# A fused attention and gated feed-forward kernel: another written order for tiles 3 to 8, with multiplies and block sums shared otherwise between VectorE and GpSimd

## The chip, the cores and the metric

The kernel runs on one core of a Trainium2 chip. Its time is device microseconds of one execution. The engines are TensorE (PE: matmuls; PEld: its weight loads), VectorE (DVE), ScalarE (ACT), GpSimd (POOL) and SyncE (SP, which only issues transfers). ACT and POOL issue transfers too, each in its own queue and in the order written. The median of three runs before the change is 351.02 us (351.01 to 351.19).

## The reference

Blockwise causal attention over 8 batches and 8 heads, 576 positions of 64 numbers, in blocks of 64; then a feed-forward layer with a gate over all 4608 tokens.

```python
scores = scale * np.matmul(q, k.transpose(0, 1, 3, 2))
mask = block_i >= block_j                    # blocks of 64 positions
attn = softmax(np.where(mask, scores, -1e9))
x = heads_side_by_side(np.matmul(attn, v))   # 4608 x 512
gate = np.maximum(x @ w_gate, 0.0)           # w_gate, w_val: 512 x 1536
out = (gate * (x @ w_val)) @ w_out           # w_out: 1536 x 512
```

(The names softmax and heads_side_by_side stand for a few lines of numpy.) Inputs and output are float32.

## The kernel before

The feed-forward layer is done in nine tiles of 512 tokens: tile j below 8 has the first 512 positions of batch j, and tile 8 the last 64 positions of all eight batches. Attention for batch j+1 is done in the same stretch as tile j of the feed-forward layer, so that TensorE has matmuls of the one while the other engines finish steps of the other. Tiles 0 to 2 are written in ORDER_0 (line 64), which the change leaves alone. Tiles 3 to 6 all follow ORDER_3_6 (line 85), tile 7 ORDER_7 and tile 8 ORDER_8; tiles 7 and 8 have no attention beside them.

An order is a list of short names. The loop at the end of the kernel calls do(name) for each (line 1417), and each call writes some instructions, so the list sets the order of every engine's queue: nothing is rearranged afterwards. A star and a number repeat a name. A name in a dictionary ONLY is written in tile 6 alone, and loads for a later batch (l, w, d) are left out in tile 6. These names matter here:

- g5, v5 and the like (plain, line 1327): one of four steps of a gate or value block, a matmul of 128x512. r is its relu on ACT (line 1325), h its multiply on DVE (line 1426).
- p, a pair number n from 0 to 5, then 1 to 7: one half of one of seven block products that stand for the eight of a pair of gate and value blocks (times, line 1339; matmuls of 128x256 at line 1354). Their results go through PSUM and are put together by pair (line 1372): a, u and w are copies from PSUM to SBUF on ACT (line 1376); d, e and c add a PSUM block to an SBUF one on DVE (line 1380); r is a relu on ACT. H multiplies relu and value into hT (line 1392; both inputs in SBUF; DVE, or POOL if its name is in ON_POOL), and L does relu and multiply in one on DVE (line 1396).
- X and Y: sums of blocks of x, both inputs in SBUF (x_sums, line 1162; DVE or POOL). U: sums of weight blocks (line 979).
- s and four digits: sums of blocks of hT that the output products need (make_part, line 1020; both inputs in SBUF; DVE or POOL).
- M1 to M7: the seven products of the output matrix, each in six steps of two matmuls (line 1061). oa, ou, ow and oy copy the results out on ACT (line 1106), od, oe and oc add on DVE (line 1100), S0, S1, S2 issue the stores of 256 KB from ACT's queue (line 893; line 906 in tile 8, where the stores are shared out among ACT, SP and POOL). P issues the store that the tile before left over.
- A and a number: the score matmuls of one pair of heads (visit, line 608; matmuls at line 631). E and that number with t, u, f or s: its four exponentials on ACT (lines 643 and 636). C: the zeros in the corners of the exponentials (line 1507 on DVE, 1510 on POOL). V: the products with v for one head (lines 779 and 793). N: its normalisation on DVE, a reciprocal and two multiplies (lines 716, 718, 725). T: the transposing transfer of the result into x, from SP's queue (line 862). K and k: scores of the last keys and their exponential.
- l and w: loads of q, k and v of the batch after the next, issued by POOL (line 509; each issue takes it 0.62 to 0.96 us). d: the transposing transfers of q and k from SP's queue (line 519 and after).

PSUM has eight banks of 512 columns: two pairs called sc, one called one, three called ffnp. SLOTS (line 44) says by hand which buffer each use takes. A matmul that begins a new block in a bank waits until the last reader of the earlier block has finished. That is why a late copy, exponential or add holds up TensorE. PAIR_BANK, OUT_BANK and AV_BANK (lines 140, 181, 190) choose the bank for each product. on() picks the engine by the set ON_POOL (line 170):

```python
    def on(name):
        return nc.gpsimd if name in ON_POOL else nc.vector
```

Of the kernel before, what the change touches and what calls it, by code (L numbers as in the profile page):

```python
# [17 lines left out]
def kernel(  # L18
# [24 lines left out]
    OBS = 5  # L43
    SLOTS = {
        "sc": (
            "010101010101010010101010101010101010101010101010101010101010011011001001"
            "010100110110010010101001101100100101010011011001001010011101100"
        ),
        "ffnp": (
            "021021021020210210210210210210120210120202010101210120201201120120210211"  # L50
            "201021102101020120120120121201202101202101202101210221200102021010101212"
            "011210020101202020212102212001020210101012120112100201012020202121010200"
            "21210121202011"
        ),
        "ob": (
            "043210432104314013240324103420340213241302341234120324031234023402132413"
            "023412342134120142103421"
        ),
        "gate_sb": (
            "021021021021021021021021021021021021021210201202012102121020120201210212"  # L60
            "02102102"
        ),
    }
    ORDER_0 = """
# [36 lines left out]
        p06 p0w p04 p17*2 p04 p21 p1u p0u p0e p21 p05 p15 p05 p1w p14 p31 p22 p15 p14
        p0d p03*2 p2a p22 p0r p0L p1d p31 p3a p26*2 p2c p1e p1L p13*2 p1r p27 p32 p27
        p36 p51 p37 p1H p2u p2w p37 p36 p32 p51 p3c p25*2 p2d p24 p3u p24 p2e p5a p3w
        p35 p41 p35 p3d p2L p41 p23*2 p2r p56*2 p5u p34*2 p3e p4a p3L p33*2 p3r p3H
# [8 lines left out]
        p0w p0d p1u p2a p14*2 p1e p15*2 p1d p1L p02 p03*2 p0r p26 p04 p0H p02 p31 p0c
        p31 p04 p0e p26 p13 p22 p32 p13 p0L p3a p2u p1r p22 p2c p1H s0102 p27*2 p25 p37
        p25 p2w p2d p37 P p3w p24 p36 p24 p2e p2L p36 p41 p3u s0002 p32 p3c p23*2 p2r
        p51 p41 p34 p51 p4a p35*2 p3d p34 p5a p47 p42 p56 p47 p4w p46 p33*2 p42 p3r p3e
# [43 lines left out]
        (7, 3): ('one', 'sc', 'ffn'),  # L160
        (7, 4): ('ffn', 'one', 'ffn'),
        (7, 5): ('sc', 'ffn', 'sc'),
        (8, 0): ('sc', 'ffn', 'one'),
        (8, 1): ('ffn', 'ffn', 'one'),
        (8, 2): ('sc', 'ffn', 'sc'),
# [4 lines left out]
    ON_POOL = set(  # L170
        """
        32H 3C00 3C10 3C11 3C21 3C31 3X4 3X5 3X7 3s0102 3s0302 3s1002 3s1302
        3s2202 42H 4C00 4C10 4C11 4C21 4C31 4X4 4X5 4X7 4s0102 4s0302 4s1002
        4s1302 4s2202 52H 5C00 5C10 5C11 5C21 5C31 5X4 5X5 5X7 5s0102 5s0302
        5s1002 5s1302 5s2202 62H 6C00 6C10 6C11 6C21 6C31 6X4 6X5 6X7 6s0102
        6s0302 6s1002 6s1302 6s2202 70H 72H 7X4 7X5 7X7 7Y5 7Y6 7s0102 7s1002
        7s1102 7s1202 7s2302 80H 81H 82H 83H 8s0102 8s1102 8s1202 U05 U06 U07
        U43
        """.split()
    )  # L180
# [858 lines left out]
    def seven_products(j, quads, sums):  # L1039
# [45 lines left out]
        def products(which):  # L1085
# [229 lines left out]
    def program(j):  # L1315
# [101 lines left out]
        def do(t):  # L1417
# [390 lines left out]
```

## Time and profile before

| what | value |
|---|---|
| median of three runs | 351.02 us |
| the profiled execution's own time | 350.91 us |
| its span, first to last instruction | 349.1 us |
| DVE instructions, busy | 562, 245.8 us |
| ACT instructions, busy | 348, 211.4 us |
| POOL instructions, busy | 248, 201.4 us |
| tile 3 starts, last matmul ends | 138.83 us, 343.87 us |

The profile page gives busy time by engine, 40 equal slices of the span, the chain of work that ended last, and the costliest groups of instructions. In a group or in the list of instructions by time, a line reads: start and duration in us, engine, line of the kernel, operation, output and inputs by the program's names, shape, count, and in brackets how long the engine was idle before and what ended that. A matmul's drawn end is modelled, and matmuls overlap in the pipeline; their starts are measured.

### The profile page before, as it was taken

The numbers are of one execution on the slowest core, as the hardware profiler recorded it, in microseconds if no ns is written. First come the engines' busy times: TensorE is split into PE (matmuls) and PEld (weight loads), VectorE is DVE, ScalarE is ACT, GpSimd is POOL, SyncE is SP. The second block draws the span as 40 slices with busy tenths as digits, with TensorE's granted clock in tenths as the row PEclk, the third lists the DMA queues.
The fourth block names the chain that finished last, engine by engine and source line by source line (L and its number), as shares of the span: only waits on it lengthen the run. The fifth ranks groups of instructions, "written<-read, shape, count | busy, mean of one in ns | idle before, by whom it ended". The sixth has DMA issues, their size and how long they took to land.

```text
span 349.1 us, 8920 instructions
## 1 busy us (share of the span) xinstructions
PE 338.3 (97%) x3518; PEld 233.4 (67%) x3518; DVE 245.8 (70%) x562; ACT 211.4 (61%) x348; POOL 201.4 (58%) x248
## 2 busy tenths in 40 slices
PE   8999999999999999999999999999999999999993
PEld 3544455545445568776867686777777798888873
DVE  4853455667538787589648973898379877986981
ACT  5933766687235862878278846786387727536630
POOL 2767556588867803885588755973525372531520
PEclk9999999999999999999999999999999999999999
DMA  8999999999999994999989997995710130002004
GB/s 242 295 353 373 355 235 269 217 131 185 183 235 81 143 180 82 179 130 90 108 162 151 92 116 146 151 125 100 151 32 2 34 100 31 32 0 92 32 17 103
DMA packets 155402, 50.06 MB, mean 143 GB/s; under 512 B 134465, under 2 KB 151745, under 8 KB 155361
## 3 DMA queue, kind: packets, MB, share of 16 engines
q1 hardware_dynamic: 77520, 32.52, 44.3%
q0 software_dynamic: 70528, 8.98, 44.0%
q10 hardware_dynamic: 7312, 8.00, 7.8%
q8 instruction: 27, 0.44, 0.6%
q14 instruction: 15, 0.11, 0.1%
HBM read 37.75 MB, written 9.44 MB: 135 GB/s over the span
## 4 chain that ended last, share of the span: by engine, by line
PE 76%; DMA 10%; DVE 4%; POOL 4%; ACT 3%; issue 1%; ACTq 0%; SPq 0%; POOLq 0%; DVEq 0%
PE ffnp L1170 11%; PE ffnp L1061 10%; PE ffnp L1354 10%; PE sc L1354 7%; PE sc L1061 6%; PE ffnp L1330 6%; PE ffnp L1273 5%; PE one L1354 4%; PE sc L631 3%; DMA stage<-in_moe_w_out_dram 3%; DMA stage<-in_moe_w_val_dram 2%; DMA stage<-in_moe_w_gate_dram 2%; PE ffnp L779 2%; PE one L631 2%; PE sc L779 1%; PE one L779 1%
## 5 line engine op out<-in xcount | busy, mean ns | idle before, releaser
L636 ACT ACTIVATE attnT<-sc 128x1024 bf16<-128x1024 f32 x56 | 56.8, 1037 | 0.7 <-PE sc L631 0.7
L1170 PE MATMUL ffnp<-xT,wg 128*128 128x512 bf16 x140 | 37.8, 379 | 0.0
L1180 ACT ACTIVATE gate_sb<-ffnp 128x512 bf16<-128x512 f32 x35 | 20.5, 599 | 26.8 <-PE ffnp L1170 26.7
L1106 ACT COPY ob<-ffnp 128x512 f32<-128x512 f32 x20 | 11.8, 590 | 39.1 <-PE ffnp L1061 34.9
L1061 PEld LDWEIGHTS <-stage 128*128 128x128 bf16 x336 | 31.6, 98 | 4.9 <-DVE stage L1020 1.2
L1170 PE MATMUL ffnp<-xT,wv 128*128 128x512 bf16 x112 | 32.0, 380 | 0.0
L1354 PEld LDWEIGHTS <-stage 128*128 128x128 bf16 x288 | 27.6, 98 | 6.5 <-issue 0.4
L779 PEld LDWEIGHTS <-attnT 128*128 128x128 bf16 x640 | 26.2, 98 | 7.1 <-DVE attnT L1507 1.1
L1380 DVE TENSOR_TENSOR ob<-ffnp,ob 128x512 f32<-128x512 f32 x29 | 19.8, 683 | 15.0 <-ACT ob L1376 14.5
L1510 POOL MEMSET attnT<- 64x256 bf16 x22 | 7.3, 336 | 39.0 <-ACT attnT L636 19.7
L1190 DVE TENSOR_TENSOR hT<-gate_sb,ffnp 128x512 bf16<-128x512 bf16 x28 | 19.2, 684 | 14.9 <-PE ffnp L1170 13.3
L1061 PEld LDWEIGHTS <-hT 128*128 128x128 bf16 x252 | 24.2, 98 | 5.3 <-DVE hT L1396 1.2
L1325 ACT ACTIVATE gate_sb<-ffnp 128x512 bf16<-128x512 f32 x30 | 18.3, 609 | 14.9 <-PE ffnp L1354 11.1
L1354 PEld LDWEIGHTS <-wg 128*128 128x128 bf16 x224 | 21.6, 98 | 8.0 <-issue 2.1
L509 POOL DMA_DIRECT2D v_bf<-in_v_dram x30 | 24.8, 856 | 2.4 <-DMA q_bt<-in_q_dram 1.1
L1354 PEld LDWEIGHTS <-wv 128*128 128x128 bf16 x224 | 21.6, 98 | 5.5 <-ACT attnT L636 0.5
L1273 PE MATMUL ffnp<-wo,hT 128*128 128x512 bf16 x96 | 23.8, 379 | 0.1
L1170 PEld LDWEIGHTS <-wg 128*128 128x128 bf16 x144 | 13.4, 98 | 13.8 <-issue 0.5
L1170 PEld LDWEIGHTS <-wv 128*128 128x128 bf16 x144 | 13.0, 98 | 14.3 <-issue 1.5
L509 POOL DMA_DIRECT2D q_bf<-in_q_dram x20 | 17.9, 905 | 6.2 <-DVE recip L752 5.4
L1354 PE MATMUL ffnp<-xT,wg 128*128 128x256 bf16 x124 | 21.1, 273 | 0.0
L1330 PE MATMUL ffnp<-xT,wv 128*128 128x512 bf16 x64 | 21.1, 380 | 0.0
(227 smaller groups left out, 920.0 us busy)
## 6 DMA issues: line engine op xcount, KB each, us to landing
out_dram<-ob ACTq DMA_DIRECT2D x28, 256.0 KB, 3.4
stage<-in_moe_w_val_dram SPq DMA_DIRECT2D x6, 512.0 KB, 8.7
stage<-in_moe_w_gate_dram SPq DMA_DIRECT2D x6, 512.0 KB, 8.2
stage<-in_moe_w_out_dram SPq DMA_DIRECT2D x6, 512.0 KB, 10.5
q_bf<-in_q_dram POOLq DMA_DIRECT2D x20, 128.0 KB, 4.9
k_bf<-in_k_dram POOLq DMA_DIRECT2D x20, 128.0 KB, 5.9
v_bf<-in_v_dram POOLq DMA_DIRECT2D x20, 128.0 KB, 6.9
stage<-in_v_dram SPq DMA_DIRECT2D x19, 128.0 KB, 5.4
```

Of the source, the lines that this page charges most:

```text
L509: ins = nc.gpsimd.dma_start(dst, part_of)
L636: return lambda: nc.scalar.activation(at[:, :, lo : lo + 512], sc, AF.Exp, scale=scale)
L779: nc.tensor.matmul(av[:, p, :], at[:, col : col + 128], v_bf[b % 2][:, c, h, :], start=(p == 0), stop=(c == p), skip_group_check=True,)
L1061: nc.tensor.matmul(to, sums.of(c)[which][:, 128 * p : 128 * p + 128], right, start=first, stop=(c == 5), skip_group_check=True,)
L1170: nc.tensor.matmul(to, (wg, wv)[t][f // 4][:, c, 128 * (f % 4) : 128 * (f % 4) + 128], x[:, c], start=(c == 0), stop=(c == 3),)
L1180: nc.scalar.activation(gate_sb, gate, AF.Relu)
L1190: nc.vector.tensor_tensor(out=h, in0=gate_sb, in1=val, op=AX.mult)
L1273: nc.tensor.matmul(op, hT[f][:, 128 * s : 128 * (s + 1)], wo[f // 4][:, f % 4, n0:n1], start=(f == 0), stop=(f == 11),)
L1325: nc.scalar.activation(st[key], of, AF.Relu)
L1330: nc.tensor.matmul(to, (wg, wv)[t][f // 4][:, c, 128 * (f % 4) : 128 * (f % 4) + 128], x[:, c], start=(c == 0), stop=(c == 3),)
L1354: nc.tensor.matmul(st[key][:, 256 * k : 256 * k + 256], left[:, c, 128 * k : 128 * k + 128], right[:, c], start=new and (k, c) == (0, 0), ...
L1380: nc.vector.tensor_tensor(out=t, in0=st[n, of], in1=t, op=AX.add)
```

## The change

Three things change together, and nothing else in the code does. The orders of tiles 3 to 8 are written anew; the same names stand in them, each as often as before. ON_POOL has other members: in tiles 3 to 6 the multiply 5H, the sums s0202 and s2302, X6, and the corners C01 and C20 go to POOL, while s0102, s2202, X4, X7, C00 and C10 go to DVE; U07 goes to DVE, U45 and U46 to POOL. In tile 7 the multiplies 1H and 3H, s0002 and s0302 go to POOL and X7, Y5, Y6 and s1202 to DVE; in tile 8 s1002 takes the place of s1102 on POOL. The tables of PSUM buffers and banks are fitted to the new order.

```diff
@@ SLOTS: buffers of sc, ffnp, ob and gate_sb from tile 3 on @@
...
     ORDER_3_6 = """
-        A0 E0u X5 X7 g0 g1*3 X6 X4 g0 p12*2 p11*2 g1 g0*2 E0f E0s p1a p1c p17*2 p16 w0
-        E0t C01 r0 K k p16 p1u C00 V00 N00 U05 l0 v1*2 p15*2 p1w p1d V01 N01 l1 l2 l3 r1
-        v0 p14*2 p1e p13*2 v0 p1L P p1r w1 l4 l5 A1 E1t E1u E1s v1*2 h1 p21 p22 p21 v0
-        p2a p22 v0 U45 l6 l7 C11 w2 p1H p27*2 p31 p26 U46 w3 p2c h0 E1f C10 p26 p31
-        p37*2 p2w p24*2 p2u g8 p25 p2e p25 p2d p3a p36 g8 p36 p3u V11 p2L p23*2 p35*2
-        s0002 N11 p3w p3d U06 p2r g8 p34*2 p3e g8 r8 p32*2 p3c s0202 p3L p33*2 U07 w4
-        p2H p3r p3H A2 E2u p51*2 v8*2 p52 v8 p57 v8 p57 h8 E2t p5a p56 p52 p5c p56 E2s
-        V10 p5w p5u p54*2 p5e g9*4 p55*2 d0 E2f C20 l8 w5 N10 T1 r9 A3 E3u T0 d1 d2 v9*3
-        p5L s0102 M1 v9 p5d p53*2 E3s h9 s1102 M1*3 C21 p5r p5H E3f C30 M1 V21 s1002
-        s2102 s1202 s2002 M1 E3t V20 N21 N20 s0302 M7*2 T2 M7*3 oa M6 M7 ow C31 V31 N31
-        s2202 V30 M6 N30 M6 M4*2 M6*3 M4 U47 s2302 ou M4*3 U43 oe M5*3 T3 M5*3 od S2 S1
-        M2*6 M3 s1302 U03 M3*5 oy l9 l10 d3 oc S0
+        X5 A0 E0u E0s E0f g0*2 p12 g1 p12 g1 l0 X7 X6 X4 l1 l2 l3 p11*2 p1a g0*2 C00 p1c
+        E0t r0 g1 p17*2 p16 g1 K k p16 C01 V00 N00 v1*2 p1u p15*2 p1w p1d V01 N01 p14*2
+        p1e p1L v1 p13*2 v0*2 A1 P v1 r1 h1 p1r v0 p21 E1t E1u v0 h0 E1s p21 p2a p22*2
+        p2c p31 E1f p27 g8*2 p27 p2w p26*2 p2u U45 p1H s0002 p37 p31 p3a C10 p24*2 p2e
+        p32 p25*2 p2d l4 l5 l6 w0 l7 l8 s0202 C11 p2L w1 g8 p36*2 p3u V11 N11 p37 p3w g8
+        r8 p35*2 p3d p23*2 p2r p34*2 p3e p32 p33*2 p3r p3c A2 E2t p51*2 v8*2 p57*2 E2u
+        p52*2 p2H l9 l10 s0102 p3L p5a w2 w3 p3H s1002 p5c v8 p56 v8 h8 p56 p5w E2s C21
+        p54*2 U05 p5u p5e g9 E2f g9*3 r9 V10 N10 p55*2 p5d p5L v9*2 A3 E3t E3u v9*2 h9
+        d0 d1 T0 T1 d2 p53*2 p5r C20 U46 V20 M1 p5H s1102 N20 s2102 s2002 s1202 s2202
+        E3f V21 M1*3 M7*2 M1*2 E3s C30 M7*2 C31 N21 d3 T2 w4 s1302 s2302 U07 w5 oa M7*2
+        ow M6*2 V30 N30 M6*4 V31 N31 T3 M4*2 ou M5*6 U06 od M4*4 oe S1 M2 U03 s0302 M3*6
+        oy S0 U47 U43 M2*5 S2 oc
     """
@@ ORDER_7 and ORDER_8: their ends alone @@
-        p42*2 p52*2 p5c p4c p46*2 p57 p4u p57 p47*2 p55*2 p5w p5d p4w p45*2 p4d p44*2
-        p4e p54*2 p5e M1 p43 M2*2 p53*2 p4L p5L p0H s0002 P p43 p4r p4H p5r p5H M1*3 M2
-        M1*2 M2*2 s0202 s2002 s0102 M2 M7 oa M6 s2202 s2102 p2H s1102 s1002 s1202 M6 M7
+        p3e p3L p52*2 p3r p5u p5w p42 p5c p42 p4c p3H p55*2 p5d p46 p47 p54 p47 p4u p54
+        p5e p4w p45*2 p4d M2 p44*2 p4e p53*2 M1*2 p5L p4L p5r p43 M2 p43 p4r p5H s0202
+        p4H s2002 M1*2 M7 s1002 s1202 M1*2 M2*3 s2202 s1102 M7 M2 oa M6*6 s2102 M7*4 P
...
-        p3L p2H p46 p4u p56 p5u M2 p44*2 s0202 p4c p4e p52 p45 p57*2 p55*2 p45 p3H s1002
-        p4L p5w p5d p52 p4d p54*2 p5e p5c p5L p53*2 M1 p5r p5H p43*2 p4r p4H M7 M2 M1*5
-        oa s2002 s2202 M2 oca Sa s1202 M2*3 M6*6 ou s2102 s1102 M7*2 s0302 ocb s2302
+        s0102 p4c p46 p4u p44 p52*2 p5c p56 p44 p4e p57*2 p2H p45*2 p4d p5u p55*2 p5w
+        p5d M7 p54*2 p5e M1 p43 M1 p53*2 M2*2 p5r p4L p43 p4r p5L M1*4 oa p5H p4H s2002
+        s2202 M2*4 p3H s1002 s1102 s2302 s2102 s1202 M6*5 M7 M6 ou s0302 ocb Sb oca M7*4
...
@@ ON_POOL: its first lines, tile 3 @@
-        32H 3C00 3C10 3C11 3C21 3C31 3X4 3X5 3X7 3s0102 3s0302 3s1002 3s1302
-        3s2202 42H 4C00 4C10 4C11 4C21 4C31 4X4 4X5 4X7 4s0102 4s0302 4s1002
+        32H 35H 3C01 3C11 3C20 3C21 3C31 3X5 3X6 3s0202 3s0302 3s1002 3s1302
+        3s2302 42H 45H 4C01 4C11 4C20 4C21 4C31 4X5 4X6 4s0202 4s0302 4s1002
...
-    AV_BANK = {0: ('ffn', 'one'), 1: ('sc', 'sc'), 2: ('ffn', 'sc'), 3: ('ffn', 'one')}
+    AV_BANK = {0: ('ffn', 'one'), 1: ('sc', 'sc'), 2: ('ffn', 'ffn'), 3: ('ffn', 'sc')}
```

More of the change, by code (lines that the diff above doesn't have):

```diff
@@ L45 @@
         "sc": (
-            "010101010101010010101010101010101010101010101010101010101010011011001001"
-            "010100110110010010101001101100100101010011011001001010011101100"
+            "010101010101010010101010101010101010101010101010101010101001100100110101"
+            "10011001001101011001100100110101100110010011010110001010101"
         ),
@@ L50 @@
             "021021021020210210210210210210120210120202010101210120201201120120210211"
-            "201021102101020120120120121201202101202101202101210221200102021010101212"
-            "011210020101202020212102212001020210101012120112100201012020202121010200"
-            "21210121202011"
+            "201021102101020120120120121201202101202101202101210201021201021001001201"
+            "201020121020120020021021020102120102100100120120102012102012002002102100"
+            "0201210210021210102"
         ),
         "ob": (
-            "043210432104314013240324103420340213241302341234120324031234023402132413"
-            "023412342134120142103421"
+            "043210432104314013240312402312301243021340231230124302134023123012430213"
+            "402312302130214201240312"
         ),
         "gate_sb": (
-            "021021021021021021021021021021021021021210201202012102121020120201210212"
-            "02102102"
+            "021021021021021021021021021021021021021201012010212102120101201021210210"
+            "21021021"
         ),
@@ L98 @@
+        p54*2 U05 p5u p5e g9 E2f g9*3 r9 V10 N10 p55*2 p5d p5L v9*2 A3 E3t E3u v9*2 h9
[3 more added lines that the diff above has]
+        oy S0 U47 U43 M2*5 S2 oc
     """
     ORDER_7 = """
-        p11*2 p1a p01 p02 p01 X5 X7 X6 p07 p0a p12 p07 p12 X4 p1c p02 p0c Y5 p16 p06 p16
@@ L101 @@
[L101 to L104, printed above, removed]
-        p42*2 p52*2 p5c p4c p46*2 p57 p4u p57 p47*2 p55*2 p5w p5d p4w p45*2 p4d p44*2
-        p4e p54*2 p5e M1 p43 M2*2 p53*2 p4L p5L p0H s0002 P p43 p4r p4H p5r p5H M1*3 M2
@@ L107 @@
-        M1*2 M2*2 s0202 s2002 s0102 M2 M7 oa M6 s2202 s2102 p2H s1102 s1002 s1202 M6 M7
-        M6*4 ou M7*4 ow M5*5 M4 M5 s0302 s1302 od S2 M4*5 oe M3*2 s2302 M3 S1 M3 Y7 Y6
-        oc M3*2 oy S0
+        X5 p11*2 p1a p01*2 p0a X7 X6 p21 p02 p12*2 p1c X4 p07*2 p16 p02 p06 p0c p16 p06
+        p0w p04*2 p21 p22 p0u p0e p1u p05*2 p0d p22 p15 p17 p0L p2a p2c p17 p15 p1w p1d
+        p03*2 p26 p0r p0H p31*2 p14 p27 p3a p27 p14 p1e p13 p37 p13 p1r p1H s0002 p1L
+        s0102 p36 p26 p36 p32*2 p3c Y5 p51*2 p37 p2u p25 p2w p25 p2d p24*2 p2e p5a p56
@@ L110 @@
+        p3u p35*2 p23 p41 p23 p41 p3w p3d p2r p2H p34*2 p57 p33*2 p57 p56 p2L p4a p46
+        p3e p3L p52*2 p3r p5u p5w p42 p5c p42 p4c p3H p55*2 p5d p46 p47 p54 p47 p4u p54
+        p5e p4w p45*2 p4d M2 p44*2 p4e p53*2 M1*2 p5L p4L p5r p43 M2 p43 p4r p5H s0202
+        p4H s2002 M1*2 M7 s1002 s1202 M1*2 M2*3 s2202 s1102 M7 M2 oa M6*6 s2102 M7*4 P
+        ou M5*6 s2302 Y7 s0302 s1302 ow od S2 M4*5 oc M4 oe M3*6 oy S1 S0 Y6
     """
     ORDER_8 = """
-        p01*2 p11*2 p12 p0a p17*2 p1a p1w p07*2 p06*2 p12 p21*2 X4 p1c p16*2 p0u p05*2
@@ L113 @@
[L113 to L116, printed above, removed]
-        p3L p2H p46 p4u p56 p5u M2 p44*2 s0202 p4c p4e p52 p45 p57*2 p55*2 p45 p3H s1002
-        p4L p5w p5d p52 p4d p54*2 p5e p5c p5L p53*2 M1 p5r p5H p43*2 p4r p4H M7 M2 M1*5
@@ L119 @@
-        oa s2002 s2202 M2 oca Sa s1202 M2*3 M6*6 ou s2102 s1102 M7*2 s0302 ocb s2302
-        M7*3 ow M5*4 Sb M5*2 od s1302 S2 M4*6 M3*6 oy S0 oe S1
+        X4 p01 p17 p07 p21 p01 p07 p11*2 p17 p12 p21 p12 p0a p06 p1a p1c p06 p16*2 p0w
+        p04*2 p0u p05 p0e p05 p0d p1u p15*2 p1w p14 p1d p14 p1e p1L p31*2 p02*2 p0c p03
+        p2a p3a p03 p0r p0H p13*2 p1r p1H p26*2 p2u p27*2 p0L p41*2 p32*2 p3c p25 p36
+        p2w p25 p36 p2d p24*2 p2e p4a p3u p37 p22*2 p2c p37 p23*2 p3w p2r p51*2 s0002
@@ L121 @@
+        p2L p35*2 p3d p42 P p5a p34*2 p3e p3L p42 p47*2 p4w p33*2 p56 p46 p3r s0202
+        s0102 p4c p46 p4u p44 p52*2 p5c p56 p44 p4e p57*2 p2H p45*2 p4d p5u p55*2 p5w
+        p5d M7 p54*2 p5e M1 p43 M1 p53*2 M2*2 p5r p4L p43 p4r p5L M1*4 oa p5H p4H s2002
+        s2202 M2*4 p3H s1002 s1102 s2302 s2102 s1202 M6*5 M7 M6 ou s0302 ocb Sb oca M7*4
+        M5*5 ow M4 M5 M4*3 od S2 M4*2 s1302 M3*4 Sa M3*2 oy S0 oe S1
     """
@@ L156 @@
         (6, 5): ('ffn', 'one', 'ffn'),
-        (7, 0): ('ffn', 'ffn', 'ffn'),
-        (7, 1): ('sc', 'sc', 'one'),
+        (7, 0): ('ffn', 'one', 'sc'),
+        (7, 1): ('sc', 'sc', 'ffn'),
         (7, 2): ('ffn', 'ffn', 'ffn'),
[L160 to L165, printed above, removed]
+        (7, 3): ('one', 'ffn', 'sc'),
+        (7, 4): ('sc', 'ffn', 'one'),
+        (7, 5): ('sc', 'ffn', 'ffn'),
+        (8, 0): ('sc', 'one', 'one'),
+        (8, 1): ('ffn', 'ffn', 'ffn'),
+        (8, 2): ('sc', 'ffn', 'one'),
         (8, 3): ('ffn', 'ffn', 'one'),
         (8, 4): ('sc', 'sc', 'one'),
-        (8, 5): ('ffn', 'one', 'ffn'),
+        (8, 5): ('ffn', 'ffn', 'ffn'),
     }
@@ L171 @@
         """
-        32H 3C00 3C10 3C11 3C21 3C31 3X4 3X5 3X7 3s0102 3s0302 3s1002 3s1302
-        3s2202 42H 4C00 4C10 4C11 4C21 4C31 4X4 4X5 4X7 4s0102 4s0302 4s1002
[L174 to L178, printed above, removed]
+        32H 35H 3C01 3C11 3C20 3C21 3C31 3X5 3X6 3s0202 3s0302 3s1002 3s1302
+        3s2302 42H 45H 4C01 4C11 4C20 4C21 4C31 4X5 4X6 4s0202 4s0302 4s1002
+        4s1302 4s2302 52H 55H 5C01 5C11 5C20 5C21 5C31 5X5 5X6 5s0202 5s0302
+        5s1002 5s1302 5s2302 62H 65H 6C01 6C11 6C20 6C21 6C31 6X5 6X6 6s0202
+        6s0302 6s1002 6s1302 6s2302 70H 71H 72H 73H 7X4 7X5 7s0002 7s0102 7s0302
+        7s1002 7s1102 7s2302 80H 81H 82H 83H 8s0102 8s1002 8s1202 U05 U06 U43
+        U45 U46
         """.split()
     )
-    OUT_BANK = {(2, 'v'): 'ffn', (2, 'w'): 'ffn', (2, 'x'): 'one', (3, 'v'): 'sc', (3, 'w'): 'ffn', (3, 'x'): 'sc', (4, 'v'): 'sc', (4, 'w'): 'ffn', (4, 'x'): 'sc', (5, 'v'): 'sc', (5, 'w'): 'ffn', (5, 'x'): 'sc', (6, 'v'): 'sc', (6, 'w'): 'ffn', (6, 'x'): 'sc', (7, 'v'): 'ffn', (7, 'w'): 'ffn', (7, 'x'): 'one', (8, 'v'): 'one', (8, 'w'): 'sc', (8, 'x'): 'one'}
+    OUT_BANK = {(2, 'v'): 'ffn', (2, 'w'): 'ffn', (2, 'x'): 'one', (3, 'v'): 'sc', (3, 'w'): 'one', (3, 'x'): 'ffn', (4, 'v'): 'sc', (4, 'w'): 'one', (4, 'x'): 'ffn', (5, 'v'): 'sc', (5, 'w'): 'one', (5, 'x'): 'ffn', (6, 'v'): 'sc', (6, 'w'): 'one', (6, 'x'): 'ffn', (7, 'v'): 'sc', (7, 'w'): 'ffn', (7, 'x'): 'ffn', (8, 'v'): 'one', (8, 'w'): 'ffn', (8, 'x'): 'one'}
     UP_MEM = {
```

## The prediction

> **What bounds the kernel now.** I read the busy line and the 40 slices of the page first, then the shares of the chain, then the busy time of each tile of work, and last the instructions in order of time around the places where TensorE comes late.
>
> ```profile
> PE 338.3 (97%) x3518; PEld 233.4 (67%) x3518; DVE 245.8 (70%) x562; ACT 211.4 (61%) x348; POOL 201.4 (58%) x248
> ...
> PE   8999999999999999999999999999999999999993
> ...
> PEclk9999999999999999999999999999999999999999
> ...
> PE 76%; DMA 10%; DVE 4%; POOL 4%; ACT 3%; issue 1%; ACTq 0%; SPq 0%; POOLq 0%; DVEq 0%
> ```
>
> TensorE (PE) is the bound: busy 97%, clock granted in full. So the change can only remove or add gaps between matmuls. 97% hides small gaps, since a matmul is drawn about 0.16 us longer than the step to the next one. I therefore count steps from start to start. Rows of "x4" 128x256 matmuls of mean 0.273 last 0.60, a step of 0.109; 13 of 128x512 last 2.81, a step of 0.216; ten 128x65 last 0.48, a step of 0.03.
>
> Tiles 3 to 6 hold 196 of the first (21.4 us), 32 of the second (6.9), 120 of the third (3.6), four score visits of 0.77 (3.1) and last_keys (0.1): about 35.2 us. Tiles 7 and 8 hold 252 of the first: 27.5. The stretches from the start of one tile to the next:
>
> ```profile
> core 0: us, PE busy (x) PEld busy (x) DVE busy (x) ACT busy (x) POOL busy (x), PEclk, DMA share, GB/s
> 138.83:175.33 36.50, 36.23 (x417) 27.54 (x417) 26.66 (x60) 24.67 (x41) 24.73 (x30) 1.00 1.36 128
> 175.33:212.37 37.04, 36.52 (x417) 27.50 (x418) 27.61 (x62) 24.75 (x41) 27.21 (x32) 1.00 1.37 132
> 212.37:249.65 37.28, 36.58 (x418) 27.48 (x418) 27.57 (x62) 24.85 (x41) 25.96 (x31) 1.00 1.27 128
> 249.65:286.23 36.58, 36.28 (x418) 27.63 (x418) 29.00 (x66) 24.75 (x41) 16.48 (x19) 1.00 0.19 48
> 286.23:315.09 28.86, 28.29 (x255) 24.38 (x253) 23.99 (x39) 15.04 (x28) 11.73 (x10) 1.00 0.11 38
> ```
>
> Lost against these sums: 1.3, 1.8, 2.1, 1.4 and 1.4 us, and 1.3 in tile 8 (315.09 to the last matmul's end at 343.87): 9.3 us, all that the written order can win. Of it 7.0 us stand at few places, named below; 2.3 are scattered.
>
> **What late means here.** The first matmul of p11 in tile 4:
>
> ```profile
> 175.44 0.58 ACT L1106 COPY ob<-ffnp 128x512 f32<-128x512 f32 x1 [4.22 <-PE ffnp L1061]
> ...
> 176.05 0.38 ACTq L893 DMA_DIRECT2D out_dram<-ob  x1
> ...
> 176.48 0.60 ACT L643 ACTIVATE attnT<-ffnp 128x512 bf16<-128x512 f32 x1 [0.46 <-PE sc L631]
> 176.97 1.94 ACT L636 ACTIVATE attnT<-sc 128x1024 bf16<-128x1024 f32 x2
> ...
> 177.19 0.60 PE L1354 MATMUL ffnp<-xT,wg 128*128 128x256 bf16 x4
> 178.04 0.60 PE L1354 MATMUL sc<-xT,wg 128*128 128x256 bf16 x4 [0.25 <-ACT attnT L636]
> ```
>
> Four matmuls from 177.19 would let the next start at 177.63; it starts at 178.04, 0.41 late, because its PSUM bank is freed by an exponential that stands behind oy (0.58) and the issue of the store S0 (0.38) on ACT. The second kind of delay is two engines that meet:
>
> ```profile
> 193.26 1.23 DVE L1020 TENSOR_TENSOR stage<-stage,hT 128x512 bf16<-128x512 bf16 x1
> ...
> 194.48 1.63 POOL L1020 TENSOR_TENSOR stage<-hT 128x512 bf16<-128x512 bf16 x1
> ...
> 195.02 1.64 DVE L1392 TENSOR_TENSOR hT<-gate_sb,ob 128x512 bf16<-128x512 bf16 x1
> ```
>
> A block sum (L1020) takes 0.42 on DVE elsewhere and 1.16 on POOL, a multiply (L1392) 0.68 on DVE. Here the multiply p3H beside POOL's sum s0102 takes 1.64, and A3, behind it on DVE, is 0.39 late (g9 just before, 0.19). The Trainium skill ("SBUF — State Buffer", section "Who interferes with whom") says that a VectorE instruction with two SBUF inputs contends with a GpSimd instruction that reads SBUF, and whichever issues first holds the port to its end; these three lines agree.
>
> **The change, part by part.** No matmul is added or removed, and tiles 0 to 2 are untouched. I count each wait of PE as a chain: the matmul that releases the first operation, the operations in their written order, the matmul that waits. Operations queued back to back start 0.08 (DVE) or 0.12 (ACT) before the earlier one's drawn end. On the old order this gives 0.44 for p11 (measured 0.41), 0.18 for A1 (0.18), 1.18 in tile 7 (1.19) and 1.00 in tile 8 (1.02), so I use it on the new one.
>
> 1. *Start of tiles 4 to 6.* Old: M3 ends, then oy 0.59, S0 0.38, E0u 0.60, E0f 1.03, while PE has 2.46 us up to p11; short by 0.44. New: M2*5 and S2 stand between; oy, S0, S2 (0.38), E0u, E0s against 3.33 us of PE: slack 0.02. last_keys (K), 0.13 late in each of these tiles, gets slack 0.11. Lost now 3 x 0.54 = 1.6; I leave 0.1. **-1.5.**
> 2. *A1.* Its second bank waits for p15, p1d 0.69, three steps of N01 (0.19, 0.42, 0.21), p1e 0.69. The new order has one more half of v (0.216) between: from 0.18 late to 0.03 to spare, four tiles. **-0.7.**
> 3. *g9 and A3.* Lost now 0.19 twice, and 0.40, 0.39, 0.39, 0.19: 1.75. s0202 goes to POOL and earlier in the order, s0102 to DVE, so that POOL's queue near p3H holds load issues (l9, l10, w2, w3) and no sum in tiles 3 to 5; DVE also gives away p5H (0.68). Multiplies beside load issues kept 0.68 (p1H in tiles 3 to 5). The chains to A3 get slack 0.36. I leave 0.1 in all. **-1.65.**
> 4. *V11, the added wait.* Corner C11 now stands on POOL behind s0202: A1, E1t 0.60, E1u 0.60, E1s 1.03, p2a 0.59, p2c 0.69, p1H 0.69, s0002 0.42, then POOL 1.15 and 0.31, against 5.93 us of PE: short by 0.12. The old tile 5 lost 0.37 at the same matmul, behind load issues. Queued behind C11 on POOL: w1 and 2H, both with over 2 us to spare. Bounds 0 and, if s0202 takes the 1.63 that s0102 took, 0.6 a tile. I take 0.17, near the counted chain. 0.68 against 0.37: **+0.3.**
> 5. *5H on POOL.* p53, p5r 0.60, 5H 1.16, s2102 0.42, M7: slack 0.11; on DVE 5H cost 0.68. M7 loses 0.09 a tile now. Bounds 0 and 1.4 a tile (third rival); I take 0.14, since nothing that reads two SBUF tiles is written beside 5H on DVE but s1102, which ends before it. **+0.2.**
> 6. *X4 and X7 to DVE, X6 to POOL.* DVE's sums of 0.42 now stand beside the load issues l1 and l2, as s0202 did beside l8 and w5 when it took 1.23. Bounds 0 and 0.8 each; DVE has over 1 us with nothing to do before p1c (waiting for E0u, E0s, E0f and p1a), which covers either end: **0**. Uncovered it would be 0.8 a tile.
> 7. *Tile 7.* Up to M6 the new chain is p54, seven long DVE operations (0.69, step 0.60), four sums (step 0.34), with ends and semaphores 6.1 us against 5.34 of PE: 0.78 for 1.19. **-0.4.**
> 8. *Tile 8.* Old: nine long and three short operations from p44, 7.2 against 6.21. New: seven long and two short from p45, 5.55 against 5.12: 0.44 for 1.02. **-0.6.**
> 9. *Transfers.* Transposes T2 and T3 land 3.4 to 4.0 after issue; the new chain to p12 (V31, two steps of N31, T3, landing) keeps 2.2 us. d0 and d1 (4.5 and 1.8 of SP's queue) now stand ahead of T0 on SP, and T0 is still over 5 us early. The last stores keep their number, size and order (landing 2.0 to 2.7 after issue): **0**.
>
> Sum: -1.5 - 0.7 - 1.65 + 0.3 + 0.2 - 0.4 - 0.6 = -4.35. The profiled execution took 350.91 us (span 349.1 and 1.8 around it), the median of the runs is 351.02: **346.7 us**.
>
> **Rivals.** *Half of it is eaten by GpSimd's new queue.* V11 waits for POOL, and s0202 shares the port with whatever DVE does: at the upper bound of step 4 it is 0.6 - 0.17 = 0.43 a tile more, with tile 6, where s2202 meets s1302 (+0.47), 2.2 us: 348.9. For it speaks the 0.37 of tile 5, against it that DVE has only PSUM-fed adds (p2e, p2d) beside s0202; those kept 0.67 to 0.69 in all 84 cases.
>
> *The order only trades stalls.* The waits with counted slack of 0.02 to 0.11 (p11, K, A1, M7, four tiles, some sixteen places) each come 0.25 late: +4: within 0.2% of 351.0. Against it: the old order has seven places of 0.00 to 0.12 in each tile (p27, p34 to p36, p33, A3, M5), and only A3, where GpSimd meets DVE, shows a gap.
>
> *Slower: the shared port at the end of the tile.* If 5H on POOL runs a little later than counted it meets s2102 and, in turn, s1302 meets s2202 and s1102; each of these sums then takes 1.24 instead of 0.42, and V30, behind them on DVE, comes 1.43 late: 4 x 1.4 = 5.7 us: 352.4. It decides the sign from 1.1 us a tile. By the skill's rule above, read strictly, every such meeting costs the whole of GpSimd's instruction, which is this case. Against it: old s2102 and s1202 ran at 0.42 next to POOL's memset, and all three would have to meet in each tile.
>
> **How the numbers follow.** Forecast 346.7, own range 345.3 to 348.2: 0.62. First rival, 348.9 (348.2 to 350.3): 0.22. Traded stalls: 0.08. Slower: 0.08. About 0.2% (0.7 us) is what a measurement here can tell from no change. Lower end: the scattered losses of V11, M7 and tile 7 gone as well, 345.3; upper end, most of the first rival, 349.8. Faster 0.84, same 0.08, slower 0.08.
>
> **What would show it.** Tiles 3 to 6 of 35.7 to 36.1 us each, 7 and 8 of some 28.3; p11, K and A1 start without a gap; no p3H over 0.8 on DVE in tiles 3 to 5; V11's wait on POOL's L1510 in each tile at 0.1 to 0.3; M6 late by 0.8 and 0.4 in tiles 7 and 8. I am wrong if DVE's sums around s2102 take over 1 us, if V11 loses 0.5 or more, or if an xT transpose ends a wait of PE.

## The result and the profile after

The median of four runs after the change is 347.19 us (346.79 to 348.30), against 351.04 us (351.01 to 351.19) for the kernel before: a ratio of 0.9895, 95% interval 0.987 to 0.992. 3.85 us are won; 4.35 were forecast, and 347.19 lies inside the range.

The profiled execution after is the longest of the four: 348.30 us, span 346.5. From its page (the trace has 3477 of the 3518 matmuls, and all of their weight loads, by which I place them):

```profile
PE 333.9 (96%) x3477; PEld 234.0 (68%) x3518; DVE 239.8 (69%) x561; ACT 211.2 (61%) x348; POOL 202.4 (58%) x249
...
PEclk9999999999999999999999999999999999999999
...
PE 84%; ACT 4%; DVE 3%; DMA 3%; ACTq 2%; issue 2%; SPq 0%; POOL 0%; DVEq 0%
```

The clock is as before. In the chain of work that ended last PE rises from 76% to 84%, and POOL, 4% before, is gone. ACTq, which was 0%, has 2%: the queue of ACT's own transfers is on the chain now. Tiles 4, 5 and 7, from the start of each to the start of the next:

```profile
core 0: us, PE busy (x) PEld busy (x) DVE busy (x) ACT busy (x) POOL busy (x), PEclk, DMA share, GB/s
...
175.29:212.01 36.72, 35.67 (x413) 27.46 (x418) 25.74 (x61) 24.73 (x41) 25.58 (x33) 1.00 1.26 128
212.01:248.00 35.99, 35.56 (x412) 27.44 (x416) 25.75 (x61) 24.80 (x41) 24.76 (x31) 1.00 1.45 132
...
283.78:312.63 28.85, 27.97 (x254) 24.47 (x252) 25.24 (x42) 14.75 (x27) 13.47 (x11) 1.00 0.11 37
```

Tiles 3, 5 and 6 (35.95, 35.99, 35.78) are inside the promised 35.7 to 36.1. Tile 4 took 36.72, and tile 7 28.85 where 28.3 was promised. Counted from the start of tile 3 to the span's end, 210.27 us became 207.16; the stretch ahead of tile 3, which the change does not touch, was 0.51 longer in this execution.

The new losses, read as before from the distance between the starts of matmuls. At the start of tile 4:

```profile
174.92 1.68 ACTq L892 DMA_DIRECT2D out_dram<-ob  x2
...
176.65 0.60 ACT L642 ACTIVATE attnT<-ffnp 128x512 bf16<-128x512 f32 x1 [1.76 <-PE sc L630]
...
177.29 0.38 PE L1329 MATMUL ffnp<-xT,wg 128*128 128x512 bf16 x1 [0.41 <-ACT attnT L642]
...
178.21 0.60 PE L1353 MATMUL sc<-xT,wg 128*128 128x256 bf16 x4 [0.32 <-ACT attnT L635]
```

The issues of S0 and S2 take 1.68 us together (0.39 and 1.25), so E0u starts at 176.65; g1 is 0.58 late for it and p11 0.27. At the start of tile 5 the same pair took 0.38 and 0.48, and nothing waits there. At the start of tile 7 the second issue took 1.81, and p16 is 0.50 late.

The meeting of engines that the prediction showed in tile 4 is gone. DVE and POOL at the same place after:

```profile
193.80 0.54 DVE L1019 TENSOR_TENSOR stage<-hT 128x512 bf16<-128x512 bf16 x1
...
194.00 1.28 POOL L508 DMA_DIRECT2D k_bt<-in_k_dram  x2
...
194.86 0.68 DVE L1391 TENSOR_TENSOR hT<-gate_sb,ob 128x512 bf16<-128x512 bf16 x1
...
195.26 0.92 POOL L508 DMA_DIRECT2D v_bf<-in_v_dram  x1
```

The multiply p3H takes 0.68 where it took 1.64; s0102, now on DVE, takes 0.54 (2H ends on POOL 0.26 after it starts); from there until p3H has ended POOL only issues loads. The ends of tiles 7 and 8 keep one gap each, 0.71 and 0.44, for a product of the last pairs (L1395); tile 7's:

```profile
304.27 0.39 PE L1060 MATMUL ffnp<-wo,hT 128*128 128x256 bf16 x2 [0.55 <-DVE hT L1395]
```

Line numbers after the change are one lower than before.

### The profile page after: what moved, and what is told of

It reads as the page before. It is cut to its first block, busy times and chain, and to the rows that moved or that the text cites. A ratio compares the mean times of both kernels' runs of the same rounds, so it can differ in the third digit from the quotient of the medians.

```text
span 346.5 us, 8901 instructions
## 1 busy us (share of the span) xinstructions
PE 333.9 (96%) x3477; PEld 234.0 (68%) x3518; DVE 239.8 (69%) x561; ACT 211.2 (61%) x348; POOL 202.4 (58%) x249
## 4 chain that ended last, share of the span: by engine, by line
PE 84%; ACT 4%; DVE 3%; DMA 3%; ACTq 2%; issue 2%; SPq 0%; POOL 0%; DVEq 0%
PE ffnp L1169 15%; PE ffnp L1353 10%; PE sc L1353 8%; PE one L1060 7%; PE ffnp L1329 6%; PE ffnp L1060 6%; PE ffnp L1272 6%; PE one L1353 5%; PE sc L1060 4%; PE sc L630 3%; PE ffnp L778 2%; PE one L630 2%; DMA stage<-in_moe_w_val_dram 2%; ACTq L892 2%; PE sc L778 2%
## 5 line engine op out<-in xcount | busy, mean ns | idle before, releaser
L1169 PE MATMUL ffnp<-xT,wg 128*128 128x512 bf16 x130 | 36.2, 379 | 0.6
L1169 PE MATMUL ffnp<-xT,wv 128*128 128x512 bf16 x108 | 31.3, 380 | 0.2
L1272 PE MATMUL ffnp<-wo,hT 128*128 128x512 bf16 x91 | 23.1, 379 | 0.2
L642 ACT ACTIVATE attnT<-one 128x512 bf16<-128x512 f32 (+1 forms) x28 | 15.2, 543 | 10.5 <-PE ffnp L630 10.4
L1391 POOL TENSOR_TENSOR hT<-gate_sb,q_bf 128x512 bf16<-128x512 bf16 x8 | 10.2, 1285 | 19.4 <-ACT gate_sb L1324 19.3
L1105 ACT COPY ob<-one 128x512 f32<-128x512 f32 x13 | 7.6, 586 | 22.0 <-PE one L1060 22.0
L630 PEld LDWEIGHTS <-kTm 64*128 64x128 bf16 x384 | 11.4, 94 | 13.1 <-issue 7.0
```

The costliest lines, as they stand in the source:

```text
L630: nc.tensor.matmul(o, kTm[b % 2][head_of(hh), c, hp, :], qT, start=True, stop=True)
L1169: nc.tensor.matmul(to, (wg, wv)[t][f // 4][:, c, 128 * (f % 4) : 128 * (f % 4) + 128], x[:, c], start=(c == 0), stop=(c == 3),)
L1272: nc.tensor.matmul(op, hT[f][:, 128 * s : 128 * (s + 1)], wo[f // 4][:, f % 4, n0:n1], start=(f == 0), stop=(f == 11),)
```

## Experiments

Two questions: why did some issues of stores grow to two and a half to four times their length, and do steps of the prediction hold when they are undone or done alone? All kernels were timed in five rounds beside the kernel before, whose medians were 351.38, 351.25 and 351.24 us in the three groups (runs 1 to 4, 5 to 8, 9 and 10).

### 1. The changed kernel again

No edit.

> The changed kernel once more, unaltered. In its first profile the second of two stores issued back to back from ACT took 1.25, 1.81 and 1.21 us at the starts of tiles 4, 7 and 8 (0.48 at those of tiles 5 and 6), and TensorE lost 0.85 us at the start of tile 4 and 0.50 in that of tile 7 behind it. Theory: a 16 KB block of TensorE's own program is being fetched just then (175.28, 284.16, 313.27 us), and the store's issue ends only 0.40 us after the fetch. Blocks are fetched after a fixed number of matmuls, so the same three issues must be long again, and the time be near 347.2 (346.8 to 348.3). Rival: a chance delay of one execution; then the long issues are elsewhere or gone, and the time is nearer 346.8 throughout.

Measured: 347.38 us (347.10 to 347.90), ratio 0.9891 (0.9874 to 0.9907). In the trace, packets of 16 KB on the queue that the page calls "instruction" (27 in the span, one for 128 matmuls on average, with 90 to 154 between two) ran from 175.28 to 176.20, from 284.16 to 285.33 and from 313.27 to 314.25 in the first profile, and the three long issues ended 0.40 us after each. The first profile's DMA queues between 283.9 and 285.8 us, in the columns queue, packets, MB, share of 16 engines:

```profile
q8 instruction: 1, 0.02, 3.8%
```

In the second profile the start of tile 7 shows it again:

```profile
282.70 2.33 ACTq L892 DMA_DIRECT2D out_dram<-ob  x2
...
285.77 0.38 PE L1353 MATMUL sc<-perm,stage 128*128 128x256 bf16 x2 [0.44 <-ACT ob L1375]
```

Here the block came from 283.21 to 284.63, the second issue (1.92) ended 0.40 later, and p16 is 0.60 late. At tile 4 the block came 0.85 earlier (174.43 to 175.51): the second issue took 0.48, and nothing waits. At tile 8 a block came from 312.85 to 313.88:

```profile
312.20 0.93 ACTq L892 DMA_DIRECT2D out_dram<-ob  x2
```

These are two issues of 0.38, the second from 312.75 to 313.13, and so beside the block and yet not held. So the blocks come near the same places, but up to 0.95 us apart in the two executions, and not every block beside a second store makes it long: the theory held for tile 7 and failed for tiles 4 and 8. Tile 4 took 35.94 us this time.

### 2. The second store issued earlier

```diff
-  od M4*4 oe S1 M2 U03 s0302 M3*6 oy S0 U47 U43 M2*5 S2 oc
+  od M4*4 S2 oe S1 M2 U03 s0302 M3*6 oy S0 U47 U43 M2*5 oc
 (tile 7)
-  oc M4 oe M3*6 oy S1 S0 Y6
+  oc M4 oe S1 M3*6 oy S0 Y6
```

> The changed kernel with the store S2 issued before oe (tiles 3 to 6) and S1 right behind oe (tile 7), so that no second store stands ahead of the exponentials and copies at the start of the next tile. Theory (the store's issue, held by a fetch of code, made 1.35 us of the profiled 348.30): no gap over 0.1 at g1 and p11 of tile 4 and at p16 of tile 7; 346.8 to 347.0 in a profile like the first, 345.9 to 346.8 as a median. Rival (the gap came from the exponential itself, or the slower executions differ only in their first microseconds): the gap at p11 stays at 0.3 or more and the time within 0.3 us of the changed kernel's.

Measured: 346.02 us (345.83 to 346.13), ratio 0.9848 (0.9835 to 0.9862): 1.2 to 1.4 less than the two medians of the changed kernel, and all four times within 0.3 us. No gap is left at the starts of tiles 4 to 7; tile 7 takes 28.30 us.

### 3. The program code shifted

```diff
-            "j0": lambda: [junk(3, 128), junk(7, 512), junk(3, 128)],
+            "j0": lambda: [junk(3, 128), junk(28, 128), junk(3, 128)],
```

> The changed kernel with 7 idle matmuls of 512 columns at its start split into 28 of 128 columns (3.0 us either way), so that TensorE's program is 42 instructions longer and every block of its code is fetched about 21 matmuls (some 2 us) earlier; nothing else changes. Theory: the fetches near the starts of tiles 4, 7 and 8 come at about 173, 282 and 311 us, the second stores there take 0.48, and the gaps of 0.85 and 0.50 are gone: 0.8 to 1.4 us faster than the changed kernel in executions like the profiled one. Rival (fetches have nothing to do with it): the long issues stay at the starts of tiles 4, 7 and 8, and the time stays.

Measured: 346.52 us (346.21 to 346.94), ratio 0.9864 (0.985 to 0.9877), 0.7 to 0.9 less than the unshifted kernel. The blocks came at 172.08, 281.64 and 310.71, and the same pair of stores at the start of tile 7 reads:

```profile
282.69 0.92 ACTq L892 DMA_DIRECT2D out_dram<-ob  x2
```

The edit leaves the work from tile 0 on as it was, and the 2.33 us are 0.92. In run 2 no second store stands at these places, in run 3 no block runs beside one, and in both the gaps are gone. So a block that comes while ACT issues two stores in a row can hold the second one, and made these gaps; tile 8 of run 1 shows that it does not always do so. That the packets are TensorE's code is inferred from the queue's name, their pace, and their shift with 21 more matmuls.

### 4. The old order with the sums shared anew

```diff
 ON_POOL, tiles 3 to 6 of the kernel before
-  s0102
+  s0202
```

> The kernel before with one part of the change alone: in tiles 3 to 6 s0202 on POOL and s0102 on DVE, in the old order. My step 3 (the multiply p3H meets POOL's sum s0102): p3H takes 0.68, A3 loses nothing in tiles 3 to 5, and some 1.2 to 1.7 us are won: 349.3 to 349.9, less whatever s0102, now on DVE ahead of p5d, costs there (0.42 each, to 1.23 beside load issues). Rival (GpSimd's queue only shifts: 2H, pushed behind s0202 by 1.15 us, meets p3H instead, and both want SBUF): p3H stays above 1.2 and nothing is won, 350.7 to 351.3.

Measured: 350.50 us (350.23 to 350.90), ratio 0.9973 (0.9961 to 0.9984): 0.9 won. Both were half right:

```profile
192.40 1.18 POOL L1392 TENSOR_TENSOR hT<-gate_sb,ob 128x512 bf16<-128x512 bf16 x1
...
193.00 1.14 DVE L1396 SCALAR_TENSOR_TENSOR hT<-ob,ob 128x512 bf16<-128x512 f32 x1
```

p3H takes 0.68 (at 194.06), but 2H is pushed back and meets p3L, which takes 1.14. In tiles 3 to 5 A3 still loses 0.2 instead of 0.4, g9 loses nothing, and p53 loses 0.12 anew in tiles 3 to 6: 1.0 won and 0.5 lost. So the sharing alone wins 0.5 by these gaps and 0.9 by the medians, of the 1.65 that step 3 has for sharing and order.

### 5. Two more places

```diff
-  l4 l5 l6 w0 l7 l8 s0202 C11 p2L
+  l4 l5 l6 w0 C11 l7 l8 s0202 p2L
...
-  v0*2 A1 P v1 r1 h1 p1r v0 p21
+  v0 v1 A1 P v0 r1 h1 p1r v0 p21
```

This and the next three kernels start from run 2's (346.02 us).

> The kernel with the early store (346.02 us) and two more moves in tiles 3 to 6: the corner C11 is written before the loads l7, l8 and the sum s0202, and the last step of v1 before A1 instead of behind it, a step of v0 taking its place. Theory: V11's 0.12 in tiles 3 to 5 was POOL's sum s0202 ahead of C11, and p22's 0.14 in tiles 3 to 6 was the multiply h1, which waits for the last step of v1 and frees p22's bank; both gaps go, 0.9 us less: 344.9 to 345.4. Rival: what waits is only moved (C11 late behind an exponential, the loads l7 and l8 0.3 later; A1's exponentials a matmul later): within 0.3 us of 346.0.

Measured: 345.58 us (345.47 to 346.60), ratio 0.9845 (0.9831 to 0.9858). The gaps at V11 and p22 are gone, and TensorE is busy 98%:

```profile
PE 335.5 (98%) x3518; PEld 233.7 (68%) x3518; DVE 240.1 (70%) x561; ACT 211.3 (61%) x348; POOL 201.7 (59%) x249
```

Tiles 3 to 6 take 35.78, 35.71, 35.70 and 35.61 us against 35.94, 35.87, 35.87 and 35.71: 0.6 less, where the gaps were 0.9. The rest came back in steps below 0.08, and the medians show 0.4. It has the lowest median here, a little above the range expected. Against run 2 the intervals of the ratios overlap, so the claim that it is shorter rests on the two traces.

### 6. 5H on DVE again

```diff
 ON_POOL
-  35H, 45H, 55H, 65H
```

> The kernel with the early store, with the multiply 5H of tiles 3 to 6 on DVE again (my step 5 undone). Theory: 5H on POOL fed s2102 in time and took 0.68 off DVE's queue; on DVE it stands with N20 ahead of s2102, which comes about 0.5 us later, and M7 waits for it: 0.4 to 0.6 us a tile, 347.6 to 348.4. Rival, as my step 5 had it (POOL's 1.16 against DVE's 0.68 costs 0.05 a tile): 0 to 0.4 us faster, 345.6 to 346.0.

Measured: 347.57 us (347.42 to 347.70), ratio 0.9895 (0.9881 to 0.9908): 1.55 lost.

```profile
201.41 0.42 DVE L1019 TENSOR_TENSOR stage<-hT 128x512 bf16<-128x512 bf16 x1
...
202.31 0.21 DVE L724 TENSOR_TENSOR xtail<-ffnp,recip 64x64 bf16<-64x64 f32 x1
...
202.44 0.74 DVE L1019 TENSOR_TENSOR stage<-hT 128x512 bf16<-128x512 bf16 x2
...
202.90 0.28 PE L1060 MATMUL sc<-wo,stage 128*128 128x256 bf16 x1
```

With 5H ahead of them, N20's three steps end at 202.5 and s2102 starts at 202.44; M7 loses 0.30 in each of the four tiles, 1.2 of the 1.55. The rest goes with p11 of tile 4 (0.24, behind a held store) and p13 of tile 5 (0.24).

### 7. M2 ahead of M3 again

```diff
-  S2 oe S1 M2 U03 s0302 M3*6 oy S0 U47 U43 M2*5 oc
+  S2 oe S1 M2 U03 s0302 M2*5 M3*6 oy S0 U47 U43 oc
```

> The kernel with the early store, with all six steps of M2 ahead of M3 again in tiles 3 to 6, so that oy and the issue of S0 have 1.09 us less of matmuls before the next tile (my step 1 undone, S2 still early). Theory: g1 and p11 of tiles 4 to 6 wait for E0u and the exponentials behind it, 0.4 to 0.7 us a tile, and tile 7 loses little: 347.2 to 348.2. Rival (the two issues of stores were all of it, and the early one alone repairs the start of a tile): no gap at p11, within 0.3 us of 346.0.

Measured: 348.26 us (348.00 to 348.39), ratio 0.9914 (0.99 to 0.9927): 2.24 lost. The price is a little over the range, and the place was not the one expected: A0 itself waits for the copy oy, which empties its bank, 0.74 late in tiles 4, 5 and 6 (2.22 in all):

```profile
175.63 0.27 PE L630 MATMUL one<-qTm,kTm 64*128 64x256 bf16 x1 [0.67 <-ACT ob L1105]
```

Behind it p11 loses nothing more. So the wait of p11 that step 1 counts is not what this run shows.

### 8. The sums shared as before, in the new order

```diff
 ON_POOL, tiles 3 to 6
-  s0202
+  s0102
```

> The kernel with the early store, with s0202 of tiles 3 to 6 on DVE and s0102 on POOL again (the sharing of my step 3 undone, the new order kept). By my step 3 (sharing): p3H meets POOL's s0102 again and takes 1.6, A3 and g9 lose 0.4 and 0.2 a tile, 347.0 to 348.0. Rival (the order does it): POOL's queue now has l9 and l10 between 2H and s0102, so p3H is over before s0102 starts and keeps 0.68; V11 is free of s0202; 345.5 to 346.1. A third: s0202 on DVE beside the loads l7, l8 takes 1.23 and delays 2L and N11, without a price for TensorE.

Measured: 349.16 us (348.80 to 349.23), ratio 0.9938 (0.9926 to 0.9951): 3.14 lost, more than my step 3 allows. g9 is 0.72 to 0.78 late in tiles 3 to 5:

```profile
193.91 1.28 POOL L508 DMA_DIRECT2D k_bt<-in_k_dram  x2
...
194.43 2.50 DVE L1391 TENSOR_TENSOR hT<-gate_sb,ob 128x512 bf16<-128x512 bf16 x1
...
195.21 1.16 POOL L1019 TENSOR_TENSOR stage<-hT 128x512 bf16<-128x512 bf16 x1
```

p3H starts 0.78 us before s0102, needs 0.68 alone, and yet ends at 196.93, 0.56 after s0102's end (196.37). The rest of the 3.14 stands elsewhere. DVE has s0202 again (0.42, not held, but 2L and N11 queue behind it), and p34 is 0.15 late in tiles 3 to 6 and p33 0.07 to 0.13, and V21 0.37 in tile 6, while V11's 0.12 is gone. The rival's reckoning, that p3H would be over by then, fails; so does the third guess, in the 1.23 and in being without a price. The Trainium skill ("SBUF — State Buffer", section "Who interferes with whom") gives the port to whoever issues first. By the recorded starts that is p3H, and it is the one that waits: the start that a profile draws does not tell who has the port. A new theory: a GpSimd sum that is ready and stands in POOL's queue behind the issues of loads holds the port while those issues still run.

### 9. The same, with the sum behind one that is not ready

```diff
 from run 8's kernel
-  p2H l9 l10 s0102 p3L p5a w2 w3 p3H s1002 p5c
+  p2H l9 l10 p3L p5a w2 w3 p3H s1002 s0102 p5c
```

> The kernel of the run before (s0202 on DVE, s0102 on POOL, 349.16 us, where p3H took 2.50 us although it started 0.78 us ahead of s0102) with s0102 moved behind s1002 on POOL, a sum that waits for p3H. The loads l9, l10, w2, w3 stay on POOL beside p3H. Theory: a GpSimd sum that is ready, and stands in POOL's queue behind the issues of loads, has the port already while those issues run; with s0102 behind s1002 nothing ready stands behind the loads, p3H takes 0.68, g9 loses nothing: 345.9 to 346.6. Rival: the issue of a load itself holds VectorE; p3H, beside l9, l10, w2, w3 as before, stays over 1.2 and g9 loses 0.3 or more a tile: 347.3 to 349.

Measured: 346.69 us (346.12 to 347.30), ratio 0.9864 (0.9848 to 0.988), 0.1 above the theory's range and 0.6 below the rival's.

```profile
193.66 1.28 POOL L508 DMA_DIRECT2D k_bt<-in_k_dram  x2
...
194.19 0.68 DVE L1391 TENSOR_TENSOR hT<-gate_sb,ob 128x512 bf16<-128x512 bf16 x1
```

The loads stand beside p3H as in run 8, at the same distance (p3H starts 0.52 after l9); only the ready sum behind them is gone, and 2.50 is 0.68. g9 loses nothing. p34 and p33 are late as in run 8 and V11 is not: 0.6 in all, which is nearly the whole distance to run 2 (0.67).

### 10. One move in the old order

```diff
 in the kernel before
-  p5L s0102 M1 v9 p5d p53*2 E3s h9 s1102 M1*3 C21 p5r
+  p5L M1 v9 p5d p53*2 E3s h9 s1102 M1*3 C21 s0102 p5r
```

> The kernel before with one move alone: in tiles 3 to 6 the sum s0102, on POOL as it was, is written behind the corner C21, so that POOL's queue has C21 (waiting for an exponential) and no ready sum behind the loads l8 and w5. Theory (as for the run above): in tiles 3 to 5 s0202 falls from 1.23 to 0.42 and p3H from 1.63 to 0.68, both still beside the issues of l8 and w5; g9 loses nothing and A3 0.2 or less: 0.6 to 1.4 us, 349.9 to 350.7. Rival (the issues of these 128 KB loads hold the port): s0202 stays near 1.2 on DVE, p3H comes after them, 0 to 0.5 us.

Measured: 351.85 us (351.57 to 352.12), ratio 1.0013 (1.0004 to 1.0022). The durations came as the theory has them, in all of tiles 3 to 5:

```profile
192.97 0.95 POOL L509 DMA_DIRECT2D k_bf<-in_k_dram  x1
...
193.35 0.41 DVE L1020 TENSOR_TENSOR stage<-stage,hT 128x512 bf16<-128x512 bf16 x1
...
193.91 0.64 POOL L509 DMA_DIRECT2D v_bf<-in_v_dram  x1
...
194.29 0.68 DVE L1392 TENSOR_TENSOR hT<-gate_sb,ob 128x512 bf16<-128x512 bf16 x1
```

s0202 takes 0.41 and p3H 0.68, beside l8 and w5. The time did not follow, because the sums on POOL moved back by a place, and s0302 now meets p5L:

```profile
198.77 1.14 POOL L1020 TENSOR_TENSOR stage<-hT,stage 128x512 bf16<-128x512 bf16 x1
...
199.13 1.33 DVE L1396 SCALAR_TENSOR_TENSOR hT<-ob,ob 128x512 bf16<-128x512 f32 x1
```

p53, which waits behind p5L on DVE, loses 0.45 in each of four tiles (1.8), against 0.2 won at A3 in three and 0.19 at g9 in two (1.0). The sum, 0.8 slower, is near the 0.6 measured.

## Why the prediction was right, and where not

All in us; the gaps of the two profiles of the changed kernel are set against those of before (7.0 named).

| step | forecast | first profile | second profile |
|---|---|---|---|
| 1 p11, K | -1.5 | -0.8 | -1.5 |
| 2 A1 | -0.7 | -0.7 | -0.7 |
| 3 g9, A3 | -1.65 | -1.75 | -1.75 |
| 4 V11 | +0.3 | 0.0 | 0.0 |
| 5 M7 | +0.2 | -0.4 | -0.4 |
| 6 X4, X7 | 0 | 0 | 0 |
| 7 tile 7's end | -0.4 | -0.5 | -0.5 |
| 8 tile 8 | -0.6 | -0.4 | -0.6 |
| p22 (not counted) | 0 | +0.6 | +0.6 |
| p16 (not counted) | 0 | +0.5 | +0.6 |
| sum | -4.35 | -3.45 | -4.25 |
| tiles 3 to 8, start to span's end | | -3.1 | -4.1 |
| span | | -2.6 | -3.6 |

The last two rows differ by the 0.5 that both executions lost ahead of tile 3. That the sums come so close is in part luck: V11 and M7 came out 0.9 better than forecast, p22 and p16, which were not counted, 1.1 to 1.2 worse. Steps 2, 7 and 8 were not undone singly; they rest on the gaps in the traces.

- **Step 1, start of tiles.** The gain came: p11 and K start without a gap in the second profile, but for 0.07 at p11 of tile 4. Run 7 takes the matmuls behind oy away and loses 2.24, so they are needed; but there A0 waits for oy, and not p11 for an exponential, so that the counted chain itself was not put to the test. The term that failed is S2's issue, which I counted at 0.38 with a slack of 0.02 behind it. It takes 0.48 behind S0, and 1.25 to 1.92 when a block of code is fetched. That cost 0.85 in tile 4 of one profile, and by the same cause p16 in tile 7, where I had looked only at the tile's end.
- **Step 2, A1.** Right: no gap in any tile.
- **Step 3, g9 and A3.** Right in size, no p3H over 0.68 in tiles 3 to 5. The reason given was too simple. Of the three lines that the prediction calls in agreement with the rule of the port, s0202 does not fit: it started 1.22 ahead of s0102 and yet took 1.23. Loads beside p3H are not harmless as such: in run 8 the same loads stand there with a ready sum behind them, and p3H takes 2.50. In the new order the next sum in POOL's queue, s1002, waits for p3H itself, so nothing can hold it. Run 8, without the sharing, takes 3.1 away; run 9, also without it but with s0102 one place later, only 0.7. So what counts in the new order is that no ready sum stands behind the loads, and not the sharing as such.
- **Step 4, V11.** The chain was right: short by 0.12, measured 0.13, in tiles 3 to 5. In tile 6, without loads ahead of the sum, nothing waits. I had taken 0.17 in four tiles.
- **Step 5, 5H on POOL.** The sign was wrong in this order. M7 loses nothing, and run 6 loses 1.55 with 5H on DVE. I had set POOL's 1.16 against DVE's 0.68 and left out what stands between: on DVE 5H pushes N20's three steps, and s2102 queues behind them.
- **Step 6, X4 and X7.** Right: X7 took 1.02 in tile 3 of the first profile beside X6, and TensorE waits for neither.
- **Steps 7 and 8, the ends of tiles 7 and 8.** Sizes 0.71 for 0.78 and 0.44 for 0.44. The matmul that waits is M1's step with the last two pairs and not M6: the long DVE operations are over before the four sums. In the first profile p06 lost 0.14 besides.
- **Step 9, transfers.** No transpose ended a wait. "The last stores keep their number, size and order" overlooked that the issue of a store occupies ACT, at the start of a tile too.
- **The floor.** The terms listed for tiles 3 to 6 add up to 35.1 and not 35.2, so some 9.7 us instead of 9.3 stood above the sums. No step of the forecast is taken from it.

The place that I did not count, p22, is a chain of the same kind: the last step of v1, h1 0.69, p22's bank, 0.14 late in four tiles. Run 5 removes it. It stands where the order is new and no gap was before, so that a list of the old gaps could not show it.

Of the rivals, the first asked for 0.6 a tile at V11 and s2202 meeting s1302 in tile 6; V11 lost 0.13, and s2202 took 0.42. The traded stalls, 0.25 at sixteen places, did not come: p22 alone is such a place. The slower one needed s2102 to meet 5H: s2102 starts as 5H ends, and the sums around it take 0.42.

## What to carry to other kernels

Count the new chains over the whole of a new order, and not only at the places that were late in the old one; a place with a slack of 0.02 behind a transfer's issue has none. When a block sum moves between VectorE and GpSimd, look at which ready GpSimd sum stands next in the queue, behind loads too, since moving one meeting made another in runs 4 and 10. Issue a store while its engine has nothing to do, rather than behind another store on the way to the first work of the next tile.

## What the runs showed of the hardware

- **Blocks of code can hold a store that follows another.** Right behind another, an issue of 256 KB from ACT took 0.48 to 0.73 us where no block came. In the twelve profiles 35 issues in tiles 3 to 8 ran beside a block. In 24 of them the issue before had ended 0.55 us or more ahead of the block, and they kept 0.38 to 0.43. Of the other 11, six took 0.87 to 1.92 and ended 0.40 to 0.43 after the block (in run 6 this was one that came 1.03 after the store before it); three of 0.40 to 0.64 ended just as long after it; two in run 1, of 0.48 and 0.38, were not held. The 21 more matmuls at the start moved the blocks earlier by 1.6 (tile 7) to 2.4 us (tile 4) against run 1. Why the first issue passes, and why those two did, is open.
- **Behind the issues of loads, a ready GpSimd sum goes with a longer VectorE operation, before the sum's own start is drawn** (2.50 against 0.68 in runs 8 and 9; s0202 1.23 against 0.41 in the kernel before and run 10). That the port is taken at the loads is inferred from these pairs; no view shows the port itself. One thing does not fit: in run 8 p3H waited until the sum was over, but in the kernel before s0202 ended at 194.49, as the sum's drawn start began (194.48).
- **What a meeting costs**: where the sum or multiply on GpSimd had started first, the held operation of 0.68 ended 0.55 to 0.56 us after it (p3L after 2H in run 4, p3H after s0102 in the kernel before; p3H in run 8 too, though drawn first). So the price is the time to GpSimd's end, less some 0.12.
- **The first microseconds vary.** The trace's first record of the full clock stands at 4.0 to 4.4 us in five profiles and at 5.8 to 7.1 in seven; tile 3 began at 138.67 to 139.09 in the five and at 138.94 to 139.57 in the seven. The same code runs up to there in all but run 3.
